# The order of loads and stores at the head of a fused transformer-block kernel: x in other parts, weights behind the transposed tiles, one store ahead of others

## The chip, the cores and the metric

The kernel runs on one core of one Trainium2 chip. The metric is the device time of one execution in microseconds (us); lower is better. Before the change the median of three runs is 823.29 us (822.75 to 823.58).

The core's engines appear under the profile's names: PE (matrix multiply), PEld (its weight load), DVE (vector), ACT (activation), POOL (general purpose) and SP, which here only issues transfers. A "q" behind a name (SPq) is that engine's instruction queue.

## The reference

The program computes the output of a pre-norm block and the gradients of its input and five weight matrices. All tensors are bf16; S = 2048 rows, D = 640, 32 heads of 20, F = 1728.

```python
def _A_ref(x, wqkv, wo):                       # linear attention
    qkv = (x @ wqkv) ...                       # q, k, v per head
    phi = lambda t: jnp.where(t > 0, t + 1, jnp.exp(t)) + 1e-6
    pq, pk = phi(q), phi(k)
    kv = jnp.einsum("bhsd,bhse->bhde", pk, v)
    z = jnp.einsum("bhsd->bhd", pk)
    num = jnp.einsum("bhqd,bhde->bhqe", pq, kv)
    den = jnp.einsum("bhqd,bhd->bhq", pq, z)[..., None] + 1e-6
    return (num / den ...) @ wo
def _B_ref(x, w1, w3, w2):                     # gated MLP
    return (silu(x @ w1) * (x @ w3)) @ w2
h  = x + _A_ref(_layernorm(x), A_wqkv, A_wo)
h2 = h + _B_ref(_layernorm(h), B_w1, B_w3, B_w2)
# outputs: h2, and by jax.vjp with grad_out the gradients of
# A_x, A_wqkv, A_wo, B_w1, B_w3, B_w2
```

## The kernel before, in words

S is cut into 16 tiles of 128 rows. D is five chunks of 128. The order of every engine's instructions is written out by hand; the framework adds the waits. No instruction overtakes another on its own engine.

The head is the stretch up to about 98 us. Three parts of it matter here.

**First pass over the tiles** (line 527, up to about 50 us). For tile t, DVE takes the statistics (`stat`, line 480, instructions of line 147), POOL makes the reciprocal deviation (line 154), and DVE or ACT normalises the tile in place (`p1_norm`, line 246; ACT for tiles 10, 12 and 14, by `on_act`). Tiles below 8 are transposed by PE (`p1_tr`) and copied by ACT (line 259). From tile 8 on the transposition is a DMA that SP issues (line 250) into `pqT`. Then PE multiplies by the k weights (`p1_mm`, line 267), ACT takes exp and relu (`phi`, lines 294 and 295), and DVE merges them in a held-back step (`rest`, lines 298 and 299), which stands as `R` in the table `v_steps` (line 508). There "S" is `stat`, "N" a norm ahead of `phi`, and "A", "B" and "L" are norms behind `phi`: "A" ahead of that iteration's `q_tile`, "B" and "L" behind it. `q_tile` does the same for the queries at iterations 6, 7, 9 and 11. All results in matrix form go to two PSUM buffers named `big`, used in turn.

SP issues x in parts (`load_x`, line 185) and the q, k and v weights in column ranges (`load_wq`, line 182: k is 2 to 4, q is 0 to 2, v is 4 to 6). The table `trickle` (line 505) hangs further weight loads on iterations: `w13` (line 499) lists loads of `w1` and `w3` for chunks (0,2), (2,4), (4,5) in the order w1, w3, w1, w3, w1, w3, and a last narrow one. `outs` (line 522) hangs stores on iterations: `group_out` stores four tiles of phi(k), `xn_out` four tiles of normalised x.

**Sums over the tiles** (lines 585 to 636, about 50 to 73 us). PE builds the matrix phi(k)^T x (`m_part`, `m_end`), whose rows SP transposes into `mT` (line 441). `kvT_block(m)` (line 443) multiplies the v weights by `mT`; block 1 needs the transposed rows of parts 1 and 2, block 2 those of parts 2 and 3. `r_T` (line 383) has the scaled query tiles transposed.

**Attention output and start of the MLP** (line 945, about 73 to 98 us). The last six query tiles (`q_late`), the product of kv and wo (`f2_wT`, transposed into `Wp`), x plus attention (`f2_half`), its layer norm (`f2_hn`, `f2_ht`), and then the MLP (`mlp`, line 783: gate by `w1`, sigmoid on ACT in line 793, up by `w3`). `q_out` (line 724) is a store, issued by POOL, of query tiles 10 to 13 from the buffer `pkx` to `pq_d`. The pool that holds `pkx` is released in line 955, and the MLP's tiles lie in the same memory, so the first sigmoid waits until `q_out` has read it.

What waits for a DMA waits for its semaphore. There are eight semaphores for the transfers that SP and ACT issue, used in turn, and a transfer waits until the one eight before it has landed.

The end of the kernel (line 1553) computes the gradients of w1 and w3 in blocks of columns; ACT copies each result out and issues its store, at first in two halves.

Of the kernel before, what the change touches and what calls it, by code (L numbers as in the profile page):

```python
# [9 lines left out]
P = 128  # L10
# [8 lines left out]
S, D, H, F = 2048, 640, 32, 1728  # L19
DH = D // H  # L20
ST, DT = S // P, D // P
# [34 lines left out]
def kernel(  # L56
# [19 lines left out]
    V, A, T, G, SY = nc.vector, nc.scalar, nc.tensor, nc.gpsimd, nc.sync  # L76
    dma, dmaT, dmaG = SY.dma_start, SY.dma_start_transpose, G.dma_start

    def rows(ap):
        return ap.rearrange("(t p) d -> p t d", p=P)  # L80
# [101 lines left out]
    def load_wq(a, b):  # L182
        dma(out=wqkv[:, :, a * HD:b * HD], in_=wq_v[:, :, a * HD:b * HD])

    def load_x(a, b):
        dma(out=x_sb[:, a:b, :], in_=xS[:, a:b, :])
# [4 lines left out]
    load_x(2, 3)  # L191
    load_wq(3, 4)
    load_x(3, 4)
    load_x(4, 8)

    mask = cp.tile([P, DT, M_MAX], BF16, name="mask")

# [25 lines left out]
    def load_g2T(c):  # L223
        g2T[c] = U2.tile([P, DT, W], BF16, name="g2T", tag="g2T", bufs=2)
        dmaT(out=g2T[c][:], in_=goD[c * W:(c + 1) * W, :])

    def load_w13(c0, c1):
        def go1():
            dma(out=w1[:, c0:c1, 0:F], in_=rows(B_w1)[:, c0:c1, :])

        def go3():
            dma(out=w3[:, c0:c1, :], in_=rows(B_w3)[:, c0:c1, 0:F - FL])
        return [go1, go3]

# [95 lines left out]
    def z_diag(m):  # L330
        dz[m] = hx[:, 10, m * P:(m + 1) * P]
        V.tensor_scalar(out=dz[m], in0=ident[:], scalar1=Z[:, m:m + 1], scalar2=None, op0=ALU.mult)
# [99 lines left out]
    def m_end(m, js=(0, 1)):  # L432
        mb = mbs[:, m % 4, :]
        acc = macc[m]
        for j in js:
            A.copy(out=mb[:, j * HD:(j + 1) * HD], in_=acc[j][:, 0:HD])
        if m < 2:
            A.copy(out=Z[:, m:m + 1], in_=acc[1][:, HD:HD + 1])
            z_diag(m)
        if m < DT - 1:  # L440
            dmaT(out=mT[:, :, m * P:(m + 1) * P], in_=mb)
# [13 lines left out]
    def load_w2T(a, b):  # L455
        dmaT(out=w2T[:, :, a:b], in_=B_w2[a:b, :])
# [1 line left out]
    zero_pads()  # L458
    load_w2T(0, 2 * P)
    load_g2T(0)  # L460
    load_x(8, 12)
    load_w2T(2 * P, 4 * P)
    load_wq(0, 2)
    load_x(12, ST)
    def warm_up(n, warm):
        for _ in range(n):
            T.matmul(warm[:, 0:P], lhsT=ones[:], rhs=ones[:], start=True, stop=True, skip_group_check=True)
# [31 lines left out]
    w13 = [go for c0, c1 in ((0, 2), (2, 4), (4, 5)) for go in load_w13(c0, c1)]  # L499
    w13 += [lambda: dma(out=w1[:, :, F:FP], in_=rows(B_w3)[:, :, F - FL:F])]  # L500

    def load_wo():
        dma(out=wo[:], in_=A_wo.rearrange("(c p) n -> p c n", p=P))

    trickle = {4: w13[0], 5: w13[1], 9: lambda: load_wq(4, 6), 12: w13[2], 14: w13[3]}

    R = None
    v_steps = {1: (R, ("N", 4)), 2: (("S", 5), R, ("N", 5)), 3: (("S", 6), R, ("N", 6), ("C", 0)),
               4: (("S", 7), R, ("N", 7), ("S", 8)), 5: (R, ("N", 8), ("S", 9)), 6: (R, ("N", 9), ("S", 10)),
               7: (("S", 11), R, R, ("A", 10), ("L", 11)), 8: (("S", 12), R, R, ("S", 13)),  # L510
               9: (("N", 13), R, ("S", 14), ("B", 12)), 10: (R, R, ("S", 15)), 11: (R, ("B", 14), ("L", 15))}
    V_OPS = {"S": stat, "N": p1_norm, "C": p1_scale}

    def xn_out(g, q):
# [4 lines left out]
        sl = slice(g * TPC, (g + 1) * TPC)  # L519
        dma(out=pk_v[:, sl, :], in_=pk_all[:, sl, :])  # L520

    outs = {7: ((xn_out, 0, dma),), 8: ((group_out, 0),), 12: ((group_out, 1), (xn_out, 1, dma)), 13: ((group_out, 2),)}

    QT = (6, 7, 9, 11)
    M0 = {7: (0, 1, 2), 8: (3, 4, 5)}
# [55 lines left out]
    def r_head(t):  # L581
        r_row(t)
        r_T(t)
# [4 lines left out]
    phi_rest()  # L588
    m_part(1, (14, 15))
    m_end(1)  # L590
    load_wo()
    group_out(SC - 1)
    for go in w13[4:]:
        go()
    z_late((2, 3, 4), big())
    m_part(2, range(10))
    z_rows(((0, 1), (2, 3, 4)), ps.tile([P, 2, 512], F32, name="bigx", tag="big", bufs=2))
# [2 lines left out]
    r_prod(1)  # L600
    m_part(2, range(10, ST))
    m_end(2)
    dmaG(out=m_v[:, 0, :], in_=mbs[:, 0, :])
    r_head(0)
    r_prod(2)
# [335 lines left out]
    def kv3():  # L941
# [3 lines left out]
    run((q_late, 10, f2_mT), (q_late, 11, kv3), (phi_rest,),  # L945
        (q_late, 12, lambda: (f2_wT(0), f2_wT(1))), (q_late, 13, lambda: (f2_wT(2), f2_wT(3))),
        (f2_wT, 4), (phi_rest,), (q_late, 14), (r_T, 4), (r_head, 5), (r_prod, 7),
        (mlp_ghh, 4),
        (q_late, 15), (w2_room,), (sig_table,), (f2_half, 0, 0), (f2_half, 1, 0), (f2_half, 2, 0), (f2_half, 3, 0), (mlp_ghh, 5),
        (f2_half, 0, 1), (r_store, 4, 5), (f2_half, 1, 1), (f2_hn, 0), (r_store, 5, 6), (f2_half, 2, 1), (f2_hn, 1),  # L950
        (f2_half, 3, 1), (f2_m_out,), (q_out, 10, 14),
        (f2_half, 4, 0, True), (mlp_ghh, 6), (f2_half, 4, 1, True), (f2_half, 5, 0, True), (r_red, 6, (0,)), (f2_hn, 2), (f2_hn, 3),
        (f2_ht, 2), (f2_ht, 3), (load_w2T, 8 * P, 10 * P), (mlp_ghh, 7), (r_red, 6, (1,)), (r_inv, 6), (r_scale, 6),
        (r_T, 6), (f2_rest,), (r_red, 7), (r_inv, 7), (r_scale, 7), (r_T, 7), (r_store, 6, 7))
# [26 lines left out]
    def r_end(t):  # L981
        r_scale(t)
        r_out(t)

    r_steps = [{0: ((load_x, 6, 8),), 1: ((r4_out, 0, 2),), 2: ((r_load, 8),), 3: ((load_w2T, 10 * P, F),), 4: ((r_load, 9), (r4_out, 2, 4)),
                5: ((r_store, 7, 8),),
                10: ((xn_out, 2, dmaG),), 12: ((r_load, 10),)},
               {0: ((r_den, 8), (load_x, 8, 12)), 1: ((r_end, 8), (r_load, 11), (xn_out, 3, dmaG)), 2: ((r_den, 9),), 3: ((r_end, 9), (r_load, 12)),
# [4 lines left out]
    for c in range(SC):  # L993
# [9 lines left out]
        for fc in range(FT):  # L1003
# [8 lines left out]
            if c == 0 and fc in (5, 7, 9, 11):  # L1012
                a, b = {5: (0, 3), 7: (3, 6), 9: (6, 10), 11: (10, 13)}[fc]
# [13 lines left out]
            if c == SC - 1 and fc in (1, 2, 5, 6):  # L1027
                i = (1, 2, 5, 6).index(fc)
# [61 lines left out]
    for fc in range(FT - 1):  # L1090
        b, i = divmod(fc, 4)
# [210 lines left out]
    a, b = ST - 1, ST - 2  # L1302
# [143 lines left out]
    for t in range(ST):  # L1446
        c, i = divmod(t, TPC)
# [105 lines left out]
    for i, (f0, f1) in enumerate(blocks):  # L1553
        n = f1 - f0
        for m in range(DT):
            last = (i, m) == (len(blocks) - 1, DT - 1)
            for a, b in ((0, n - P), (n - P, n)) if last else ((0, n),):
                c = (a + b) // 2
                halves = ((a, c), (c, b)) if i * DT + m < 5 else ((a, b),)
                out = [(x + y - a, z + y - a, to) for y, w in halves for x, z, to in both_grads(m, f0 + y, f0 + w)]  # L1560
                grad_job(hnN, m, lambda t: gb[i][:, t, a:b], b - a, out, A.dma_start)
        load_block(i + 2)
# [36 lines left out]
```

## Time and profile before

| what | value |
|---|---|
| median of three runs | 823.29 us |
| the profiled execution's own time | 820.91 us |
| its span, first to last instruction | 819.1 us |
| PE busy | 814.1 us, 99% of the span |
| DVE, ACT, POOL busy | 452.4, 323.6, 130.9 us |
| share of the chain that ended last | PE 96%, DVE 2%, ACT 1% |
| HBM read and written | 47.09 and 51.13 MB |

The profiled execution is 2.38 us shorter than the median of the runs, and 1.8 us of it lie outside the span. Busy time of PE counts a matmul from its start to its modelled end, so two that overlap are not told apart from one; whether PE lost time is read from the start of one matmul to the start of the next. All times below are from the start of the span.

### The profile page before, as it was taken

Reading aid. Unit: us, or ns where it says so; the run is one execution under the profiler, and the core shown is the slowest. Engines: PE = TensorE matmul, PEld = TensorE weight load, DVE = VectorE, ACT = ScalarE, POOL = GpSimd, SP = SyncE. Lnnn points to the kernel's source line nnn. Section 1 sums busy time; section 2 is a strip of 40 time slices with the busy share of each in tenths; the row PEclk is TensorE's granted clock in tenths of the full one; section 3 lists DMA queues with packets and bytes.
Section 4 is the critical chain, followed back from the end, with each engine's and each line's share of the span. In section 5 each row is a group of like instructions: output and inputs, shape, how many; then the busy total and the mean of one; then the engine's idle time right before and its main releaser. Section 6 shows DMA issues by size and latency. Waiting matters only on the chain.

```text
span 819.1 us, 13944 instructions
## 1 busy us (share of the span) xinstructions
PE 814.1 (99%) x5420; PEld 512.8 (63%) x5420; DVE 452.4 (55%) x973; ACT 323.6 (40%) x603; POOL 130.9 (16%) x193
## 2 busy tenths in 40 slices
PE   9999999999999999999999999999999999999998
PEld 6677544555555555777777777777777777544444
DVE  7859987998898566300057777772781544200000
ACT  7856688665565666011122212222212334211111
POOL 2233333333222212100001111110220000000000
PEclk9999999999999999999999999999999999999999
DMA  9899699796485556999977877259974997967751
GB/s 264 219 290 239 166 244 327 225 245 173 127 211 156 169 170 167 222 261 226 257 176 180 211 197 200 58 107 187 287 195 93 181 194 159 239 164 186 160 141 36
DMA packets 323873, 157.88 MB, mean 193 GB/s; under 512 B 242784, under 2 KB 317056, under 8 KB 323808
## 3 DMA queue, kind: packets, MB, share of 16 engines
q1 hardware_dynamic: 281040, 116.18, 61.6%
q0 software_dynamic: 7328, 24.48, 8.7%
q10 hardware_dynamic: 35440, 16.34, 7.7%
q8 instruction: 42, 0.69, 0.4%
q14 instruction: 23, 0.19, 0.1%
HBM read 47.09 MB, written 51.13 MB: 120 GB/s over the span
## 4 chain that ended last, share of the span: by engine, by line
PE 96%; DVE 2%; ACT 1%; issue 0%; DMA 0%; POOL 0%; ACTq 0%; DVEq 0%
PE mm L394 20%; PE job L1346 20%; PE ghn L1142 14%; PE gxn L1515 8%; PE gw L1097 7%; PE o L910 4%; PE o L856 3%; PE gwo L1230 3%; PE big L267 3%; PE gr L1199 3%; PE dkv L1452 3%; PE macc L429 2%; PE at L654 2%; PE mm L267 1%; PE dkv L1380 1%; DVE st L147 1%
## 5 line engine op out<-in xcount | busy, mean ns | idle before, releaser
L1346 PE MATMUL job<-gb,hnN 128*128 128x496 bf16 (+3 forms) x576 | 116.8, 366 | 0.0
L1142 PEld LDWEIGHTS <-ggb 128*128 128x128 bf16 x864 | 84.5, 98 | 32.8
L1346 PEld LDWEIGHTS <-hnN 128*128 128x128 bf16 x576 | 55.8, 98 | 61.0
L394 PE MATMUL mm<-pqT,w 128*128 128x512 bf16 x405 | 93.8, 379 | 0.1
L394 PEld LDWEIGHTS <-w 128*128 128x128 bf16 x540 | 52.5, 98 | 63.4 <-issue 1.4
L1350 ACT CAST obs<-job 128x496 bf16<-128x496 f32 (+4 forms) x56 | 28.5, 510 | 123.7 <-PE job L1346 120.9
L1142 PE MATMUL ghn<-w13a,ggb 128*128 128x320 bf16 x448 | 63.5, 299 | 0.0
L1157 DVE SCALAR_TENSOR_TENSOR wb<-gs,hnb 128x640 f32<-128x640 bf16 x16 | 13.2, 825 | 88.7 <-ACT gs L1154 88.7
L1142 PE MATMUL ghn<-w13b,ggb 128*128 128x320 bf16 x416 | 61.4, 299 | 0.0
L394 PE MATMUL mm<-g2T,w2T 128*128 128x512 bf16 x240 | 59.6, 379 | 0.0
L1097 PE MATMUL gw<-g,hb 128*128 128x320 bf16 x416 | 56.8, 299 | 0.0
L1207 POOL TENSOR_TENSOR sz<-Zb,g_h 128x640 f32<-128x640 bf16 x16 | 20.2, 1261 | 197.7 <-DVE g_h L1208 197.7
L1097 PEld LDWEIGHTS <-hb 128*128 128x128 bf16 x416 | 40.6, 98 | 16.0 <-issue 0.3
L419 ACT CAST ghh<-mm 128x512 bf16<-128x512 f32 x48 | 28.3, 589 | 47.7 <-PE mm L394 40.1
L793 ACT ACTIVATE sig<-mm 128x512 bf16<-128x512 f32 x56 | 33.9, 605 | 26.4 <-PE mm L394 21.1
L1154 ACT ACTIVATE gs<-ghn 128x640 bf16<-128x640 f32 x16 | 11.3, 704 | 78.8 <-PE ghn L1142 73.9
L394 PEld LDWEIGHTS <-w2T 128*128 128x128 bf16 x260 | 25.4, 98 | 23.4
L267 PEld LDWEIGHTS <-pqT 128*128 128x128 bf16 x320 | 30.7, 98 | 13.7 <-ACT pqT L259 1.5
L267 PE MATMUL big<-wqkv,pqT 128*128 128x320 bf16 x250 | 38.6, 299 | 0.6 <-ACT pqT L259 0.3
L1346 PEld LDWEIGHTS <-g 128*128 128x128 bf16 x320 | 31.0, 98 | 11.5
L829 DVE TENSOR_TENSOR gate<-gate,sig 128x1024 bf16<-128x1024 bf16 x28 | 19.3, 689 | 33.2 <-ACT gate L804 30.5
L910 PE MATMUL o<-w,hhT 128*128 128x320 bf16 x224 | 35.0, 299 | 0.0
(219 smaller groups left out, 1369.9 us busy)
## 6 DMA issues: line engine op xcount, KB each, us to landing
hh_d<-hhT SPq DMA_DIRECT2D x24, 256.0 KB, 2.7
gg_d<-gate POOLq DMA_DIRECT2D x24, 256.0 KB, 4.3
gg_d<-ghh POOLq DMA_DIRECT2D x24, 256.0 KB, 3.4
ggb<-gg_d SPq DMA_DIRECT2D x6, 896.0 KB, 5.4
ggb<-gg_d ACTq DMA_DIRECT2D x6, 832.0 KB, 5.7
ggb<-gg_d SPq DMA_DIRECT2D x2, 1728.0 KB, 12.7
x_sb<-in_A_x_dram SPq DMA_DIRECT2D x5, 640.0 KB, 5.9
pk_d<-pk_all SPq DMA_DIRECT2D x4, 640.0 KB, 6.6
```

The source lines that it names most:

```text
L267: T.matmul(acc, lhsT=pqT[:, c, t * P:(t + 1) * P], rhs=wqkv[:, c, n0:n0 + HD], start=(c == 0), stop=(c == DT - 1))
L394: T.matmul(acc[:], lhsT=w[:, c, fc * P:(fc + 1) * P], rhs=rhs[:, c, :], start=(c == 0), stop=(c == DT - 1))
L419: A.copy(out=ghh[n // 2][:, n % 2, :], in_=acc[:])
L793: A.activation(sig[:, i, :], gp[:], AF.Sigmoid)
L856: T.matmul(accs[i, j][:, 0:HD], lhsT=hhT[c][:, fc, i * P:(i + 1) * P], rhs=w2[:, fc, j * HD:(j + 1) * HD], start=(first and fc == 0), stop ...
L910: T.matmul(o2["ps"][:, 0:HD], lhsT=hhT[c][:, fc, i * P:(i + 1) * P], rhs=w2[:, fc, j * HD:(j + 1) * HD], start=(fc == 0), stop=(fc == FT - 1))
L1097: T.matmul(acc[:, j, 0:HD], lhsT=hb[b][:, t, i * P:(i + 1) * P], rhs=g2[:, t, j * HD:(j + 1) * HD], start=(t == 0), stop=(t == ST - 1))
L1142: T.matmul(acc[:, j, 0:HD], lhsT=ggb[t // 2][:, k, lo:lo + P], rhs=rhs[:, j * HD:(j + 1) * HD], start=(k == 0), stop=(k == NG - 1))
L1199: T.matmul(gr[t][:, j, 0:HD], lhsT=ghT[t][:, c, :], rhs=wT2[:, c, j * HD:(j + 1) * HD], start=(c == 0), stop=(c == DT - 1))
L1346: T.matmul(acc[:, 0:n], lhsT=lhs[:, t, m * P:(m + 1) * P], rhs=rhs(t), start=(t == 0), stop=(t == ST - 1))
L1350: A.copy(out=ob, in_=acc[:, 0:n])
L1515: T.matmul(acc[:, j, 0:HD], lhsT=g, rhs=wqT[:, k, j * HD:(j + 1) * HD], start=(k == 0), stop=(k == 14))
```

## The change

SP's, POOL's and ACT's orders change; PE's and DVE's instructions keep theirs.

- x is loaded in tiles 4 to 6, 6 to 10 and 10 to 16 in place of 4 to 8, 8 to 12 and 12 to 16.
- Of `trickle`, the load of `w3` for chunks (0,2) becomes two, one on iteration 5 and one on iteration 6. The v weights move from iteration 9 to behind `m_end(1)`. The load of `w3` for chunks (2,4) moves from iteration 14 to behind the last `group_out`. `load_wo` and the last three loads of `w13` move from there to behind `m_end(2)`.
- The first `group_out` goes from iteration 8 to iteration 9. The norm of tile 14 on ACT goes ahead of iteration 11's `q_tile`.
- `q_out` goes from behind `f2_m_out` to ahead of `mlp_ghh(4)`.
- In the first pass of the MLP, `load_w2T(10 * P, F)` and `r_load(8)` change places.
- At the end, the fifth result of the first block is stored whole, no longer in two halves.

```diff
-    load_x(4, 8)
+    load_x(4, 6)
...
-        def go3():
+        def go3(c0=c0, c1=c1):
             dma(out=w3[:, c0:c1, :], in_=rows(B_w3)[:, c0:c1, 0:F - FL])
...
     load_w2T(0, 2 * P)
     load_g2T(0)
-    load_x(8, 12)
+    load_x(6, 10)
     load_w2T(2 * P, 4 * P)
     load_wq(0, 2)
-    load_x(12, ST)
+    load_x(10, ST)
...
-    trickle = {4: w13[0], 5: w13[1], 9: lambda: load_wq(4, 6), 12: w13[2], 14: w13[3]}
+    trickle = {4: w13[0], 5: lambda: w13[1](0, 1), 6: lambda: w13[1](1, 2), 12: w13[2]}
...
-               9: (("N", 13), R, ("S", 14), ("B", 12)), 10: (R, R, ("S", 15)), 11: (R, ("B", 14), ("L", 15))}
+               9: (("N", 13), R, ("S", 14), ("B", 12)), 10: (R, R, ("S", 15)), 11: (R, ("A", 14), ("L", 15))}
...
-    outs = {7: ((xn_out, 0, dma),), 8: ((group_out, 0),), 12: ((group_out, 1), (xn_out, 1, dma)), 13: ((group_out, 2),)}
+    outs = {7: ((xn_out, 0, dma),), 9: ((group_out, 0),), 12: ((group_out, 1), (xn_out, 1, dma)), 13: ((group_out, 2),)}
...
     m_end(1)
-    load_wo()
+    load_wq(4, 6)
     group_out(SC - 1)
-    for go in w13[4:]:
-        go()
+    w13[3]()
...
     m_end(2)
+    load_wo()
+    for go in w13[4:]:
+        go()
...
         (f2_wT, 4), (phi_rest,), (q_late, 14), (r_T, 4), (r_head, 5), (r_prod, 7),
-        (mlp_ghh, 4),
+        (q_out, 10, 14), (mlp_ghh, 4),
...
-        (f2_half, 3, 1), (f2_m_out,), (q_out, 10, 14),
+        (f2_half, 3, 1), (f2_m_out,),
...
-    r_steps = [{0: ((load_x, 6, 8),), 1: ((r4_out, 0, 2),), 2: ((r_load, 8),), 3: ((load_w2T, 10 * P, F),), 4: ((r_load, 9), (r4_out, 2, 4)),
+    r_steps = [{0: ((load_x, 6, 8),), 1: ((r4_out, 0, 2),), 2: ((load_w2T, 10 * P, F),), 3: ((r_load, 8),), 4: ((r_load, 9), (r4_out, 2, 4)),
...
-                halves = ((a, c), (c, b)) if i * DT + m < 5 else ((a, b),)
+                halves = ((a, c), (c, b)) if i * DT + m < 4 else ((a, b),)
```

## The prediction

> **What bounds the kernel now.** I read the page first, then the chain of waits from 0 to 110 us, then the timelines of PEld, SP and ACT there, and the list of DMA issues for single transfers.
>
> ```profile
> PE 814.1 (99%) x5420; PEld 512.8 (63%) x5420; DVE 452.4 (55%) x973; ACT 323.6 (40%) x603; POOL 130.9 (16%) x193
> ...
> PEclk9999999999999999999999999999999999999999
> ```
>
> PE is busy 99% of 819.1 us at full granted clock, and the change leaves its 5420 matmuls alone. So a gain can only come from places where PE starts a matmul late, and a loss only from new ones. The chain shows two in the head:
>
> ```profile
> 35.83 0.50 DVE pk_all L299
> 36.37 0.37 issue
> 36.73 0.70 ACT mq L294
> 37.44 0.60 ACT rq L295
> 38.08 1.52 PE big L267 x10
> ...
> 95.78 0.37 POOL m_d L712
> 96.15 2.67 DMA pq_d<-pkx
> 98.82 1.86 issue
> 100.79 0.04 issue
> 100.84 0.46 ACT sig L793
> ...
> 102.45 4.48 PE mm L394 x20
> ```
>
> The first: DVE's merge of an earlier tile releases ACT, ACT's relu frees the buffer `big`, and PE starts at 38.08. From 25 us to there the chain is DVE almost without a gap. The second: `q_out`, issued at 96.15, lands at 100.6 (4.5 us in the list of issues), and only then may the first sigmoid overwrite `pkx`; its matmul had ended at 99.10. PE then waits for ACT's copy out of its PSUM buffer. The timeline of the weight loads has the places in PE's own row:
>
> ```profile
> 38.09 1.18 PEld L267 LDWEIGHTS <-pqT 128*128 128x128 bf16 x9 [0.32 <-issue]
> ...
> 40.12 1.32 PEld L267 LDWEIGHTS <-pqT 128*128 128x128 bf16 x10
> ...
> 97.83 4.23 PEld L394 LDWEIGHTS <-w 128*128 128x128 bf16 x21 [0.46 <-issue]
> 102.45 1.61 PEld L394 LDWEIGHTS <-w 128*128 128x128 bf16 x8 [0.40 <-issue]
> ```
>
> From start to start, against the usual 0.136 us (320 columns) and 0.216 us (512), PE loses 0.28 us at 38.08, 0.16 at 97.86 and 0.28 at 102.45. The row at 40.12 lost nothing, but its tile 12 landed at 37.03 + 3.0 = 40.0: met by 0.1 us. So are tile 9 (25.81 + 4.6 = 30.46, wanted at 30.60) and tile 14 (41.79 + 2.6 = 44.36, wanted at 44.47).
>
> **x in other parts.** Tiles 6 and 7 used to land with tiles 4 and 5 at 9.70; now they come with the second part, issued in the place that SP reached at 11.25, and `stat(6)` wants them at 15.74:
>
> ```profile
> 7.08 4.12 SPq L225 DMA_TRANSPOSE g2T<-in_grad_out_dram  x1
> 11.25 0.58 SPq L186 DMA_DIRECT2D x_sb<-in_A_x_dram  x1
> ...
> 15.74 0.88 DVE L147 BATCH_NORM_STATS2 st<-x_sb 128x6 f32<-128x320 bf16 x2
> ```
>
> The 640 KB part of before took 4.8 us from there: 16.07, 0.33 us too late. But 4.12 us for `g2T`'s issue is long (2.66 at 552.70 for as many rows): SP stood behind a backlog, and that is now 320 KB smaller, 0.97 us by the old part's own pace (landings 7.76 to 9.70 for 640 KB). So it issues between 10.28 and 11.25 and lands between 15.1 and 16.07. Earlier data gain nothing, as DVE is not free before 15.74. A delay d costs little at first (the transposition of tile 6 is ready 0.49 us early) but DVE has no gap to recover in, so d arrives at 38.08 in full. Bounds 0 to +0.33; I take 0, since the row of `g2T` says that SP waited for the queue. The Trainium skill, "DMA: Bandwidth & Descriptors", section "Anatomy of one DMA", fits 2.0 us plus bytes over 436 GB/s (for POOL's transfers): an estimate of 3.5 us, landing at 14.75 even from 11.25, and so 0 at both ends. The row's 4.8 us, for SP's transfer, says that this is too short here. The last part, now 960 KB, lands some 0.9 us after the old 22.5; `stat(10)` starts at 25.70: 0.
>
> **Weights and transposed tiles.** Half of `w3`, 416 KB, leaves the place ahead of tile 9 and stands ahead of tile 10, whose 32.42 has until 34.13; 416 KB took about 1.0 us (832 KB, landings 58.03 minus 55.95). The first `group_out` no longer stands ahead of tiles 13 and 12, nor 800 KB of v weights ahead of tile 14. Margins grow by 0.4 to 1.1 us, time by 0. ACT's norm of tile 14 (0.94 us) goes ahead of the last `q_tile`'s exp and relu: its buffer frees at 41.9 and not 40.96, PE wants it at 42.43: 0.
>
> The v weights now go where `wo` was issued (55.35, 6.5 us): 61.9, for a matmul at 64.10; the slowest loads near there took 9.0 us, which would be 64.35 and cost 0.25. I take 0, from the same size in the same place. Part 2 of `mT` has only 0.4 us in hand (68.08 for 68.48) and loses `wo` and three loads from ahead of it: not later. Part 3 (68.28 + 5.5 = 73.76, wanted at 75.64) gets them ahead, 1.88 us in hand. What is really new in SP's queue there is the 800 KB, some 2.1 us, moved out of a slack stretch. Engines were 43% busy at 69 us, so it partly fills room: bounds 0 to +0.2, I take 0. `wo`, by 72 for 78, and the last w loads, by 73 for 97.83, have room. SP's issues behind them (the `r_T` tiles) are read after 85.
>
> **`q_out` earlier.** POOL reaches it behind `r_prod(7)`, at 84.42 + 1.54 = 85.96; it costs POOL 0.76 us, with its next work at 91.72. With the 4.5 us of before it lands at 90.5, well ahead of the sigmoid. The sigmoid then starts behind its matmul, near 99.15 and not 100.84; ACT's copy comes 1.7 us earlier and the 0.28 us at 102.45 go. Next in line there is PE itself. At 97.86 the transposed tile 1 took 3.4 us where 2.6 is usual; but `q_out` was issued 1.8 us behind it and two stores stay, so of 0.16 I take 0.05 (bounds 0 to 0.16).
>
> Its price is a collision where it now runs, 87 to 90 us, with the last transposition of `Wp` (85.22, 2.6 us, 1.4 us in hand) and two `r_T` tiles (over 3 in hand). Bounds 0 to +1.5: the 480 KB store issued at 68.36 made its neighbour 2.9 us late, and 2.9 minus 1.4 is 1.5. I take 0, as that store moved its bytes only about 2 us after its issue; here that is 88, when the `Wp` tile has landed (87.84). The same page, "Queues, rings and completion order", says that an engine alternates between queues packet by packet; by that rule the tile would be held at most twice its own time, under its 1.4 us, and again 0. The trace does not bear it out well: at 71 to 72 us POOL's store moved nearly all the bytes.
>
> **The rest.** The load of `w2T`'s last rows landed at 119.21 for 119.79; issued ahead of `r_load(8)` it gains room; the latter is read much later: 0. One store fewer near 716 us saves ACT a 0.34 us issue beside matmuls that do not wait: 0.
>
> **Sum.** -0.28 - 0.05 = -0.33 us: span 818.8, the execution 820.91 - 0.33 = 820.6. The median of the runs stands 2.38 above the profiled execution; I carry that over: 823.29 - 0.33 = 823.0. About 0.2%, 1.65 us, is what a measurement of this kernel tells from no change, so this is "same". The bounds, the collision aside, give 822.85 (all of the 0.16) to 823.8 (0.33, 0.25 and 0.2 on top); with the runs' own spread of 0.4 to either side the forecast's own range is 822.4 to 824.2.
>
> **Rivals.** (1) *Margins that hold only in this execution.* Tiles 9, 12, 14 and tile 1 of the MLP are met by 0.10 to 0.14 us. If the 2.38 us of the other runs are mostly such waits, growing with any slower transfer, the change removes most of them: 2.0 us, 821.3. For: all runs are slower than the profiled one, and every such margin grows. Against: 1.8 us of that execution lie outside the span too, so the difference may be the way of timing; no row shows such a wait.
>
> (2) *Slower: tile 6 late.* It decides as soon as the second x part lands after 15.74. The transfers right behind it took 6.8, 7.5 and 8.6 us; at 6.8 from 11.25 it lands at 18.05, DVE is 2.3 us late, nothing in its row makes it up, and PE loses that by 38.08: 823.29 + 2.3 - 0.33 = 825.3. Against: those stood behind this one, it stands behind less than before.
>
> (3) *`q_out` in the wrong company*: `Wp`'s tile as late as the bound says, +1.5 - 0.33: 824.5.
>
> (4) *The sigmoid is held by something else*: the 0.28 us stay, 823.3. Its other waits had ended long before, so this is unlikely.
>
> **Chances.** Forecast 0.50, (1) 0.27, (2) 0.15, (3) 0.04, (4) 0.04. Faster by over 0.2%: (1), 0.27. Slower: (2), 0.15. Within: the rest, 0.58. The range goes from 821.0, which takes in (1), to 824.8, which takes in (3) and the bounds and leaves out most of (2).
>
> **What would show it.** Right: the first sigmoid near 99.2 with no DMA in the chain ahead of it, no gap in PEld near 102.2, `q_out` at 86, `stat(6)` at 15.74 in an unbroken DVE row, 0.28 still lost at 38. Wrong: DVE waiting for x near 15.7 and over 0.3 us lost at 38; a gap of PEld at 64, 68, 75 or 89; a median more than 1.65 us away while the span moved by 0.3.

## The result, and the profile after

| what | before | after |
|---|---|---|
| median of 9 runs each, alternating | 822.86 us (821.97 to 826.29) | 820.81 us (820.24 to 822.61) |
| ratio after / before, 95% interval | | 0.9977 (0.9968 to 0.9987) |
| profiled execution: span | 819.1 us | 818.8 us |
| profiled execution: own time | 820.91 us | 820.60 us |

The change makes the kernel 2.05 us faster, which is more than the 1.65 us that can be told from no change. The profiled execution moved by 0.31 us, nearly the 0.33 us of the forecast, but out of other parts than the forecast's (below). Most of the gain is therefore in what the other executions of the kernel before do and its first profiled one did not.

The page of after: PE's busy time is again nearly the whole span (some matmul records are missing in this trace).

```profile
PE 812.4 (99%) x5393; PEld 513.0 (63%) x5420; DVE 452.7 (55%) x973; ACT 323.8 (40%) x603; POOL 130.9 (16%) x193
```

The chain of waits of after, 30 to 110 us. Both stretches shown of before are now PE alone: no DVE or ACT ahead of `big` near 38, no DMA and no ACT between the transposed rows (96.45) and the end of the first two MLP steps.

```profile
36.52 2.72 PE big L267 x20
39.23 0.82 PE macc L429 x6
...
96.45 0.45 PE trh L767 x5
96.90 5.18 PE mm L394 x24
102.13 4.48 PE mm L394 x20
```

The timeline of PE's weight loads of after. The 20 loads from 36.22 run on where 9 of them began with a gap at 38.09 before; the row at 97.60 has 30 loads without a gap. In between stands a wait that before did not have, ahead of 85.55.

```profile
36.22 2.68 PEld L267 LDWEIGHTS <-pqT 128*128 128x128 bf16 x20
...
85.55 2.57 PEld L656 LDWEIGHTS <-pqT 128*128 128x128 bf16 x20 [0.65 <-issue]
...
97.60 6.36 PEld L394 LDWEIGHTS <-w 128*128 128x128 bf16 x30
```

Three rows of the timelines of SP, DVE and ACT: the second x part is issued at 10.68 (11.25 before), tile 6's statistics start unhindered at 15.65, and the first sigmoid starts at 99.14 behind ACT's own copy (100.84 before, behind the store).

```profile
10.68 0.58 SPq L186 DMA_DIRECT2D x_sb<-in_A_x_dram  x1
...
15.65 0.88 DVE L147 BATCH_NORM_STATS2 st<-x_sb 128x6 f32<-128x320 bf16 x2
...
99.14 0.60 ACT L795 ACTIVATE sig<-mm 128x512 bf16<-128x512 f32 x1 [0.21 <-ACT x_sb L661]
```

Weight load by weight load against before, the profiled execution gains 0.09 us at the start, 0.27 at 38, loses 0.51 at 85.5 and gains 0.45 between 96 and 102. Only the last of these stood in the forecast's sum, as 0.33, so that the agreement of the totals is luck.

### The profile page after: what moved, and what is told of

Same layout as the page of the kernel before. It is cut to its first block, busy times and chain, and to the rows that moved or that the text cites. A ratio compares the mean times of both kernels' runs of the same rounds, so it can differ in the third digit from the quotient of the medians.

```text
span 818.8 us, 13921 instructions
## 1 busy us (share of the span) xinstructions
PE 812.4 (99%) x5393; PEld 513.0 (63%) x5420; DVE 452.7 (55%) x973; ACT 323.8 (40%) x603; POOL 130.9 (16%) x193
## 4 chain that ended last, share of the span: by engine, by line
PE 97%; ACT 1%; DVE 1%; issue 0%; POOL 0%; DVEq 0%; ACTq 0%
PE mm L394 20%; PE job L1348 20%; PE ghn L1144 14%; PE gxn L1517 8%; PE gw L1099 7%; PE big L267 4%; PE o L912 4%; PE o L858 3%; PE gwo L1232 3%; PE macc L429 3%; PE gr L1201 3%; PE dkv L1454 3%; PE at L656 2%; PE dkv L1382 1%; PE gp L394 1%; PE warm L467 0%
```

## The experiments

Eighteen runs were made in five groups. Each group ran on one chip with the kernel before among it (medians of before: 822.62, 822.68, 823.12, 823.13 and 823.72 us), and each run left one profile. The main reading is the same for all: the k-th weight load of the kernel's profile against the k-th of the first profile of before, and in which stretch the difference changed. The table gives these changes in us (plus is lost time; stretches by the first profile's clock; "sigmoid" is 95 to 106). "Close" is the time from the last store's landing to the end of the span, beyond the 1.2 us of before. (e4's own time is 2.15 us above its span, so that its execution did not end earlier.)

| kernel | start to 25 | tile 9, 30.6 | 38 | tile 14, 44.5 | mT, 68 | Wp, 85 to 90 | sigmoid | 107 to 540 | 540 to 568 | close | own time of that execution |
|---|---|---|---|---|---|---|---|---|---|---|---|
| before, first profile | 0 | 0 | 0 | 0 | 0 | 0 | 0 | 0 | 0 | 0 | 820.91 |
| e1_again (before) | 0.02 | 1.40 | -0.27 | 0 | 0.48 | 0 | 0.83 | 0 | 0 | 0 | 823.39 |
| h1_before (before) | 0.07 | 1.20 | -0.28 | 0 | 0 | 0 | 0.64 | 0.37 | 0.01 | 0 | 822.93 |
| e2_store | -0.02 | 1.22 | -0.28 | 0 | 0 | 0 | -0.45 | 0 | 0.01 | 0 | 821.42 |
| e3_weights | 0.33 | 0 | 0.03 | 0 | 0 | 0 | 0.90 | 0 | 0.01 | 0.41 | 822.59 |
| e4_x | 0.22 | 1.42 | -0.28 | 0 | 0.07 | 1.33 | 0.60 | 0 | 0.01 | -0.29 | 824.38 |
| after, first profile | -0.09 | 0 | -0.27 | 0 | 0 | 0.51 | -0.45 | 0 | 0 | 0 | 820.60 |
| f1_after (after) | -0.07 | 0 | -0.27 | 0 | 0 | 0 | -0.45 | 0 | 0.01 | 0 | 820.12 |
| g4_after (after) | 0.06 | 0 | -0.24 | 0 | 0 | 0 | -0.45 | 0 | 2.10 | 0 | 822.38 |
| h2_after (after) | -0.01 | 0 | -0.19 | 0 | 0 | 0.16 | -0.45 | 0 | 0.35 | 0 | 820.77 |
| f2_after_store_back | 1.68 | 0.37 | -0.09 | 0 | 0 | 0 | 0.79 | 0 | 0.52 | 0 | 824.22 |
| f3_half_w3_and_store | -0.04 | 0 | 0.01 | 0 | 0.30 | 0 | -0.45 | 1.19 | 0.01 | 0.41 | 822.35 |
| f4_after_loads_back | 0.32 | 0 | -0.15 | 2.07 | 0 | 0 | -0.45 | 0 | 0.79 | 0 | 823.52 |
| g1_x_back | -0.06 | 0 | 0.03 | 0 | 0 | 0.28 | -0.45 | 0 | 0.01 | 0 | 820.65 |
| h3_x_back_again | 0.41 | 0 | 0.03 | 0 | 0 | 0 | -0.45 | 0 | 1.53 | 0 | 822.42 |
| g2_x_and_store_back | 0.09 | 0 | 0.03 | 0 | 0 | 0 | 0.04 | 0 | 0.44 | 0 | 821.46 |
| g3_x_after_tile_six | 0.08 | 0 | 0.02 | 0 | 0 | 2.13 | -0.46 | 0 | 0.01 | 0 | 822.70 |
| h4_rows_of_x_later | 0 | 0 | 0.02 | 0 | 0 | 0 | -0.45 | 0 | 0 | 0.43 | 820.95 |
| i1_rows_of_x_close (as h4) | -0.04 | 0 | 0.02 | 0 | 0 | 0 | -0.45 | 0 | 0.01 | 0.43 | 820.89 |
| i2_half_w3_close (as f3) | 0.94 | 0 | -0.28 | 0 | 0 | 0 | -0.45 | 0 | 0.01 | 0.43 | 821.58 |

### First group: the kernel before again, and each part of the change alone

**The kernel before, unchanged.** 

> The kernel before, unchanged, once more: it tells how far two sets of runs of one kernel differ, and gives a second profiled execution. Theory M (the just-met transfers of the head turn into waits in most executions): ratio 1.000, and if the execution profiled is a usual one (span near 821, not 819.1), PE starts late by 0.2 us or more at one or several of tile 9, 12 or 14 in the first pass, at tile 1 of the MLP, or behind the first sigmoid, about 2 us in total more than in the first profile. Theory E (the extra lies elsewhere, at the start or the end of the kernel, and the change touches it by chance): ratio 1.000, the head between 20 and 110 us as in the first profile, the extra at another place.

Measured: 822.53 us (821.85 to 825.53), ratio 1.0004 (0.9995 to 1.0013). In its timeline of weight loads PE waits for tile 9, and longer at 104.91 than the first profile did at 102.45:

```profile
32.14 2.56 PEld L267 LDWEIGHTS <-pqT 128*128 128x128 bf16 x20 [1.56 <-DMA pqT<-x_sb]
...
104.91 3.98 PEld L394 LDWEIGHTS <-w 128*128 128x128 bf16 x19 [1.17 <-issue]
```

Its chain of waits names both transfers. The transposition of tile 9 was issued at 25.83 (25.81 in the first profile) but took 6.27 us and not 4.65, behind the 832 KB of `w3` issued at 24.66. The store `q_out` is issued at 97.76; the 2.67 and 2.70 us are its 5.3 us to landing.

```profile
25.83 6.27 DMA pqT<-x_sb
32.09 0.04 issue
32.14 1.94 PE big L267 x13
...
97.76 2.67 DMA pq_d<-pkx
100.43 2.70 issue
```

So the first profile of before was an execution that happened to lose little. Theory M is borne out for tile 9 and the sigmoid; tiles 12 and 14 cost nothing here. Another 0.48 us went at part 2 of `mT`, which the first profile met by 0.4.

**The store alone.**

```
-        (mlp_ghh, 4),
+        (q_out, 10, 14), (mlp_ghh, 4),
...
-        (f2_half, 3, 1), (f2_m_out,), (q_out, 10, 14),
+        (f2_half, 3, 1), (f2_m_out,),
```

> Before, with q_out alone moved ahead of mlp_ghh(4). Theory S (the store's landing holds the first sigmoid, and in most executions by much more than the 0.28 us of the first profile): most of the gain, ratio 0.998 (-1.5 us or more). Theory M (the transposed tiles): only the 0.3 us of the forecast, ratio 0.9996.

Measured: 821.89 us (821.42 to 822.33), ratio 0.9990 (0.9981 to 0.9998). That is 0.73 below before in its group, half of what theory S asked for and more than theory M's 0.3. Nothing is lost at the sigmoid, but tile 9 still costs 1.22:

```profile
31.92 2.56 PEld L267 LDWEIGHTS <-pqT 128*128 128x128 bf16 x20 [1.38 <-DMA pqT<-x_sb]
```

**The weights alone** (halves of `w3`, v weights, fourth block of `w3`, `wo` and the last w loads later, first `group_out` one iteration later, norm of tile 14 ahead of the last `q_tile`; the lines of the last two are left out here).

```
-    trickle = {4: w13[0], 5: w13[1], 9: lambda: load_wq(4, 6), 12: w13[2], 14: w13[3]}
+    trickle = {4: w13[0], 5: lambda: w13[1](0, 1), 6: lambda: w13[1](1, 2), 12: w13[2]}
...
-    load_wo()
+    load_wq(4, 6)
...
-    for go in w13[4:]:
-        go()
+    w13[3]()
...
+    load_wo()
+    for go in w13[4:]:
+        go()
```

> Before, with the moves of the w3, v, wo and w loads, the first group_out one tile later and the norm of tile 14 ahead of the last q_tile; x parts and q_out as before. Theory M: most of the gain, ratio 0.998 to 0.9985 (-1.2 to -1.7 us), PE without a gap at tiles 9, 12 and 14. Theory S: 0, ratio 1.000, with the gap behind the first sigmoid as before.

Measured: 822.40 us (821.50 to 824.34), ratio 0.9998 (0.9989 to 1.0007): 0.22 us, not theory M's 1.2 to 1.7. Tile 9 landed at 29.36 and cost nothing, as theory M said; the sigmoid cost 0.90, and 0.41 us stand at the close:

```profile
103.71 3.98 PEld L394 LDWEIGHTS <-w 128*128 128x128 bf16 x19 [1.45 <-issue]
```

**The x parts alone.**

```
-    load_x(4, 8)
+    load_x(4, 6)
...
-    load_x(8, 12)
+    load_x(6, 10)
...
-    load_x(12, ST)
+    load_x(10, ST)
```

> Before, with x loaded in tiles 4 to 6, 6 to 10 and 10 to 16, nothing else. Theories M and S: 0, ratio 1.000. The forecast's bounds: 0 to +0.33 us. If this part carries the gain (a third theory X: the statistics or g2T come sooner and DVE's unbroken chain to 38 us starts sooner), ratio 0.998.

Measured: 822.81 us (822.04 to 825.13), ratio 1.0003 (0.9993 to 1.0013): no gain. The profile loses at tile 9 and the sigmoid like the other executions of before, and 1.33 at `Wp`, with the weight loads in their old places:

```profile
88.19 2.57 PEld L654 LDWEIGHTS <-pqT 128*128 128x128 bf16 x20 [1.48 <-DMA Wp<-pkx]
```

So no part gives the whole 2 us, and the parts do not simply add: where tile 9 was late, the 0.28 us at 38 was not lost as well (e1, e2; h1 below), because PE came later to the buffer that it would have waited for.

### Second group: the change without a part, and the two parts that the first group names

**The changed kernel, unchanged.** 

> The changed kernel, unchanged, for a second profile and more runs. Theory T (the kernel before usually loses 1.2 to 1.4 us at 30.6 behind the undivided 832 KB load of w3, and 0.6 to 0.9 us at the first sigmoid behind the store of the turned queries; the changed kernel loses neither): 820.8, tile 9 lands by 29.5, no gap of PE at 30.5 or at 102, the mT tiles met, and the gap of about 0.5 us at 85.5 is there again, since SP's queue brings the Wp tile late in every execution. Theory L (luck: the one profile of the changed kernel was as lucky as the first one of the kernel before): a gap of over 0.5 us somewhere between 28 and 82, and 821.5 or more.

Measured: 820.97 us (820.12 to 823.43), ratio 0.9986 (0.9977 to 0.9995). No gap at tile 9 or the sigmoid, and none at 85.5 either: the gap there is not in every execution, against what theory T expected. Five of the twelve times lie above 822, seven below 821.3.

**The store back in its place.**

```
-        (q_out, 10, 14), (mlp_ghh, 4),
+        (mlp_ghh, 4),
...
-        (f2_half, 3, 1), (f2_m_out,),
+        (f2_half, 3, 1), (f2_m_out,), (q_out, 10, 14),
```

> The changed kernel with q_out back in its old place, all else as changed. Theory T: the store takes 0.6 to 0.9 us again at the first sigmoid, but the gap at 85.5 stays (it was SP's transposition, not the store), so 821.5 and a gap in PE near 102. Theory C (the store at 85.5 was itself what held the Wp tile): the gap at 85.5 goes, 0.5 back, so 821.0. Theory W (the store's place is worth only the 0.28 us of the first profile): 821.1 with the gap at 85.5 still there.

Measured: 821.14 us (820.58 to 824.22), ratio 0.9986 (0.9976 to 0.9995). The sigmoid costs 0.79 again in the profile, which is the slowest of the twelve executions; the lowest time is only 0.46 above that of f1, so there are executions in which the store's old place costs less than 0.5. The profile also shows what the prediction's second rival described: the second x part, issued at 10.87, landed at 18.00, and DVE and PE waited (timelines of DVE and of the weight loads):

```profile
18.02 0.89 DVE L147 BATCH_NORM_STATS2 st<-x_sb 128x6 f32<-128x320 bf16 x2 [2.23 <-DMA x_sb<-in_A_x_dram]
...
20.59 0.28 PEld L257 LDWEIGHTS <-x_sb 128*128 128x128 bf16 x5 [1.87 <-DVE x_sb L160]
```

**Before, with halves of w3 and the store alone.**

```
-    trickle = {4: w13[0], 5: w13[1], 9: lambda: load_wq(4, 6), 12: w13[2], 14: w13[3]}
+    trickle = {4: w13[0], 5: lambda: w13[1](0, 1), 6: lambda: w13[1](1, 2), 9: lambda: load_wq(4, 6), 12: w13[2], 14: w13[3]}
...
-        (mlp_ghh, 4),
+        (q_out, 10, 14), (mlp_ghh, 4),
```

> The kernel before with two parts of the change alone: the second block of w3 loaded in two halves (416 KB behind tile 8, 416 KB behind tile 9) and q_out moved. Theory T: both usual losses go, 822.6 - 1.3 - 0.7 = 820.6; and as the v weights, wo and the last w loads stay in their old places, the gap at 85.5 does not come, or seldom. Theory E (the other moved loads carry part of the gain): 821.3 or more, with gaps of PE at tiles 10 to 14 (34 to 45) or at mT part 2 (68.5).

Measured: 821.49 us (820.85 to 825.11), ratio 0.9993 (0.9983 to 1.0003): not the 820.6 of theory T. Tile 9 landed at 29.07 and the sigmoid waited for nothing, but `mT` part 2 was late by 0.30, behind `wo` and three more loads, and 1.19 us were lost near 131 to 135, which did not come back in i2 below:

```profile
68.87 0.30 PEld L448 LDWEIGHTS <-wqkv 128*128 128x128 bf16 x5 [0.46 <-DMA mT<-hx]
```

**The change with its late loads back.**

```
-    trickle = {4: w13[0], 5: lambda: w13[1](0, 1), 6: lambda: w13[1](1, 2), 12: w13[2]}
+    trickle = {4: w13[0], 5: lambda: w13[1](0, 1), 6: lambda: w13[1](1, 2), 9: lambda: load_wq(4, 6), 12: w13[2], 14: w13[3]}
...
-    load_wq(4, 6)
+    load_wo()
...
-    w13[3]()
+    for go in w13[4:]:
+        go()
...
-    load_wo()
-    for go in w13[4:]:
-        go()
```

> The changed kernel with the v weights, the fourth block of w3, wo and the last w loads back in their old places (x parts, halves of w3, q_out and the rest as changed). Theory T: the gap at 85.5 came from SP standing behind the loads that were put near 61 to 72; without them 820.3, and x(0,6) is issued before 77 and its landing is no longer at 83.5. Against it, wo and three loads stand ahead of mT part 2 again, which was met by 0.4 in one profile and missed by 0.5 and 0.2 in two: if that is the usual case 820.6 to 820.8, no better than the change. Theory P (the Wp tile is late by chance, whatever SP carries): a gap near 85.5 here too, 820.8.

Measured: 821.80 us (821.40 to 823.52), ratio 0.9992 (0.9984 to 1.0001). Worse than the change, by 0.8 us against f1. No gap at 85.5, but the v weights stood ahead of tile 14 again (issued at 39.42), and it took 5.70 us where 2.6 is usual. Its chain of waits:

```profile
41.10 5.70 DMA pqT<-x_sb
46.80 0.05 issue
46.84 1.26 PE big L267 x8
```

In the seven profiles that have the v weights there and tile 14's norm in its old place, the tile took 2.57 to 2.64 us. There its transposition was issued 3.5 to 4.5 us behind the v weights; in f4 it was 1.68, since the norm comes earlier, and the first `group_out`, now on iteration 9, stood right ahead of the weights. So tile 14 was on time in all of these; as far as one profile tells, it is the earlier norm and the later `group_out` that want the weights gone from there.

### Third group: x in its old parts

**The change with the old parts of x.** Diff: the three `load_x` lines as in before. 

> The changed kernel with x loaded in its old parts (4 to 7, 8 to 11, 12 to 15), all else as changed. Theory D (tile 6's statistics, wanted at 15.7, wait for the new second part in a share of the executions: 2.2 us and 1.7 lost by PE in one profile, 0.3 lost in two, nothing in two; so the changed kernel's times of 822.1 and more are these executions): the lowest stays at 820.1 to 820.6, hardly any time above 821.5, the median 0.2 to 0.5 lower than that of the changed kernel in the same call, 820.5, and stat(6) starts near 15.7. Theory N (the new parts relieve the queue and help the weights behind them): stat(6) near 15.7 as well, but the median 821.3 or more, with a gap at tiles 9 to 14.

Measured: 820.64 us (820.33 to 820.87, seven runs), ratio 0.9974 (0.9963 to 0.9985), with no time above 820.9. The profile loses 0.28 at `Wp` and, with the old parts, the 0.28 at 38 is there:

```profile
38.05 1.18 PEld L267 LDWEIGHTS <-pqT 128*128 128x128 bf16 x9 [0.34 <-issue]
...
85.67 2.57 PEld L656 LDWEIGHTS <-pqT 128*128 128x128 bf16 x20 [0.43 <-issue]
```

**Old x parts and the old place of the store.** Diff: that of g1 and that of f2. 

> The changed kernel with both the x parts and q_out as they were: the moved weights, the halves of w3 and the earlier norm of tile 14 are left. Theory T and D (wait at tile 9, at tile 14 and at the sigmoid): g1 plus 0.5, so 821.0; a gap near 102 of 0.6 to 0.9 us. Against it stands the run of the moved weights without the norm of tile 14, 822.4. Theory N (the new x parts are what the gain needs): 822.2 or more.

Measured: 822.21 us (821.05 to 823.71), ratio 0.9989 (0.9978 to 0.9999). That is 1.57 above g1 on the same chip, with the store's place as the only difference; the 821.0 expected was too low. (The run that the expectation sets against it, e3, had the norm of tile 14 moved as well, so g2 is e3 with the whole store at the end and the exchanged loads, and both agree: 0.91 below before here, 0.22 and the 0.43 of the close there.) Its one profile lost as little at the sigmoid as the first profile of before did (store issued 96.27, landed 4.50 us later).

**x in parts of tiles 4 to 6, 7 to 10 and 11 to 15.**

```
-    load_x(4, 6)
+    load_x(4, 7)
...
-    load_x(6, 10)
+    load_x(7, 11)
...
-    load_x(10, ST)
+    load_x(11, ST)
```

> The changed kernel with x in parts of tiles 4 to 6, 7 to 10 and 11 to 15: the first tile of the second part is wanted at 18.4 and not at 15.7. Theory D: a landing of 15.4 to 18.0 is in time, so as g1: 820.5, hardly any time above 821.5. Theory N: as the changed kernel or better, 820.8, for the parts stay spread. If both kernels with another tile 6 keep a tail above 822, that tail is not tile 6's.

Measured: 820.87 us (820.52 to 822.70), ratio 0.9977 (0.9968 to 0.9986). The median is as theory D had it, but three of eleven times are above 821.5, and the profile is one of them. It shows the third rival: `q_out`, issued at 86.00, ran together with the last transposition of `Wp`, issued at 85.97, which took 5.59 us and not 2.6; the third one was late too.

```profile
86.77 2.57 PEld L656 LDWEIGHTS <-pqT 128*128 128x128 bf16 x20 [1.40 <-DMA Wp<-pkx]
91.60 0.52 PEld L656 LDWEIGHTS <-pqT 128*128 128x128 bf16 x5 [1.12 <-DMA Wp<-pkx]
```

**The changed kernel beside them.** 

> The changed kernel on the same chip, as the measure for g1 to g3 and for a third profile: 820.9, with times in two groups, near 820.5 and near 822.3. In its profile the x part lands between 15.3 and 18; if the run is of the upper group, the 1.7 us must stand in PE between 16 and 21 (theory D) and not behind 25.

Measured: 821.28 us (820.25 to 822.55), ratio 0.9981 (0.9970 to 0.9992). Its profile is of the upper group, but against theory D not because of tile 6: x landed at 15.83, and the 2.10 us stand far outside the change, at 566, where PE waits for `tri`. The transposition it waits for was issued at 562.64 and took 5.48 us, 2.62 in the first profile of before; POOL issued a store 1.23 us behind it (timelines of SP and POOL):

```profile
562.64 1.22 SPq L1239 DMA_TRANSPOSE tri<-tri  x1
...
563.87 0.60 POOL L1354 DMA_DIRECT2D out_dram<-obs  x1 [14.14 <-ACT obs L1352]
```

### Fourth group: more profiles, and SP's queue ahead of Wp

**The kernel before again.** 

> The kernel before, unchanged, for a third profile. Theory T: 822.7; a gap of 1.2 to 1.4 us at tile 9 near 30.6 (it was there in all three executions with the undivided w3 load but the first), and 0.6 to 1.1 at the sigmoid. Theory L (the first profile is the usual one): no gap at 30.6, at most 0.28 at the sigmoid, and the rest of the 822.7 somewhere the change does not touch, for instance at 547 to 567, where other kernels lost up to 2.1 us.

Measured: 822.75 us (821.51 to 824.12), ratio 0.9997 (0.9988 to 1.0006). The third profile of before loses in the two places that the second one did (timelines of the weight loads and of ACT). Theory L falls.

```profile
31.99 2.56 PEld L267 LDWEIGHTS <-pqT 128*128 128x128 bf16 x20 [1.36 <-DMA pqT<-x_sb]
...
102.47 0.60 ACT L793 ACTIVATE sig<-mm 128x512 bf16<-128x512 f32 x1 [2.66 <-PE mm L394]
```

The matmul named there had long ended; the store had landed at 102.25.

**The changed kernel again.** 

> The changed kernel once more: 820.8 to 821.3, lowest 820.2, some 3 in 10 of the times above 822; no gap at 30.6 or at 102; if above 821.5, the loss is at tile 6 (16 to 19), at Wp (85 to 90) or at 547 to 567.

Measured: 821.15 us (820.27 to 823.55), ratio 0.9979 (0.9969 to 0.9988); three of twelve above 822, as expected. Its profile loses 0.16 at `Wp` and 0.35 at 566.

**Old parts of x again.** 

> The changed kernel with the old parts of x, again: theory D (tile 6 makes the tail) 820.6, hardly any time above 821.5, lower than h2 by 0.2 to 0.6. If the tail is Wp's or that of 547 to 567, which have nothing to do with x, it shows here too: 3 in 10 above 822, and the median that of h2.

Measured: 820.95 us (820.38 to 823.09), ratio 0.9976 (0.9967 to 0.9985), with two of eleven above 822. So the upper times are not tile 6's alone: this profile (822.42) lost 1.53 us at 566. The list of waits has it:

```profile
PE gkvT L1401 <- DMA tri<-tri: 1.4, 1, 1.4
```

**Two of six tiles of x behind the transpositions of Wp** (on top of g1).

```
-    load_x(0, 6)
+    load_x(0, 4)
...
-        (f2_wT, 4), (phi_rest,), (q_late, 14), (r_T, 4), (r_head, 5), (r_prod, 7),
+        (f2_wT, 4), (phi_rest,), (q_late, 14), (r_T, 4), (load_x, 4, 6), (r_head, 5), (r_prod, 7),
```

> As h3, and of the six rows of x that SP loads ahead of the transpositions of Wp, two (tiles 4 and 5, 160 KB) go behind them. Theory Q (Wp is late since it stands behind that load in SP's queue): the load ahead lands about 0.4 to 0.8 us sooner, Wp's third tile by 85.2 and not 85.5, the gap of 0.3 at 85.6 goes: 820.3, 0.3 under h3. Theory C (Wp's tiles are late by the store of the turned queries or by chance): the gap near 85.6 stays or moves to 91, no gain on h3.

Measured: 821.20 us (820.80 to 823.75), ratio 0.9981 (0.9973 to 0.9990). In the profile the load ahead landed at 82.35 and not 83.61 (g1), `Wp`'s third tile at 85.20 and not 85.61, and there is no gap at 85.5, as theory Q said. That alone proves little, since h3, without this edit, had none either. But the twenty profiles bear theory Q out. Corrected for the time that PE had lost or gained by then, the tiles of x loaded ahead landed at 83.54, 83.64, 83.87, 84.63 and 84.87 in the five that lose at `Wp`'s third tile (h2, g1, after, g3 and e4, which lose 0.16, 0.28, 0.51, 1.26 and 1.33), and at 83.42 or earlier in the fifteen others. The third tile landed 1.8 to 2.0 us behind them in all five. But 820.3 did not come: the lowest of twelve times is 820.80, where g1 and h3 had 820.33 and 820.38. The weight loads lose nothing more; 0.43 us stand behind the last store instead, and the fifth group asks why. Rows of SP's timeline:

```profile
77.14 1.40 SPq L186 DMA_DIRECT2D x_sb<-in_A_x_dram  x1
79.93 6.49 SPq L708 DMA_TRANSPOSE Wp<-pkx  x5
...
88.85 0.70 SPq L186 DMA_DIRECT2D x_sb<-in_A_x_dram  x1
```

### Fifth group: the time behind the last store

**The kernel of h4 again** (diff as there). 

> The kernel of h4 once more, for the time between the last store's landing and the end of the span. Theory K (it belongs to the kernel): 1.6 us again, lowest time 820.8. Theory R (it belongs to the execution): 1.2 us, and a time of 820.4 or less where the weight loads lose nothing. In both, no gap at 85.5.

Measured: 821.06 us (820.82 to 822.92, eight runs), before in this group 823.72 us, ratio 0.9970 (0.9957 to 0.9984). The span ends 1.63 us after the last landing again, which is theory K. `Wp`'s third tile lands at 85.19, and there is no gap at 85.5.

**The kernel of f3 again** (diff as there). 

> The kernel of f3 once more, for the same time at the end. Theory K: 1.6 us again, lowest time 820.8; theory R: 1.2 us. Beside it: tile 9 lands near 29.1 and costs nothing, and the 1.19 us lost near 131 to 135 in f3 show whether they come back.

Measured: 821.72 us (821.09 to 823.46, eight runs), ratio 0.9987 (0.9974 to 1.0000). 1.63 us again: theory K. Tile 9 landed at 29.03 and cost nothing; 0.94 us were lost at 14.4 to 15.4, where PE waited for `g2T`, which landed at 15.34 (13.22 in the first profile of before).

The traces' semaphore events show what the time is. At the end SP waits for all transfers in eight steps, in a fixed order of their semaphores: 101 first, then 104 to 110. In the kernel before, the change and the kernels not named below, SP and ACT issue 424 transfers, and the last store has semaphore 110. The first seven steps are then over before it lands, and one is left. In e3, f3 and h4 the halved `w3`, or the second load of x, makes it 425. The last store then has semaphore 101, SP stands at the first step until it lands, and takes the other seven behind it at 0.06 us each: 7 x 0.061 = 0.43 us. The change itself halves `w3` (one transfer more) and stores one result at the end in one piece (one fewer), so it stays at 424.

## Why the prediction was right or wrong

**The step that failed: "The median of the runs stands 2.38 above the profiled execution; I carry that over."** The 2.38 us were not a way of timing. Every execution's time stands some 1.8 us above its span, the profiled ones included (1.7 to 2.2), and the other executions of before really are longer: two more profiles of it show 823.39 and 822.93. They lose it in waits for transfers, as rival (1) had it, but only in part in those that the rival named. Tile 9, met by 0.1 us in the first profile, costs them 0.9 to 1.1 us net; tiles 12 and 14 cost nothing. The store, which already cost the first profile 0.45, costs 0.64 and 0.83 more, and one of them loses 0.48 at a part of `mT` that the first profile met by 0.4, the other 0.37 behind 107. The rival's chance was 0.27 and its time 821.3; measured 820.81, also below the range's 821.0. Of the 2.2 us between the forecast of 823.0 and this, 0.43 is the base: nine runs of before have a median of 822.86, where three had 823.29.

**Tile 9, "met by 0.1 us" and counted as 0.** The condition was right, the price was missing. With the undivided load of 832 KB the tile was late in four of five executions (e1, e2, e4, h1), by 1.20 to 1.42 us for PE; with the halves it was late in none of fifteen, landing 3.1 to 3.4 us after its issue against 6.1 to 6.3. The 0.28 us at 38 come back in exchange, unless x is in the new parts, so about 1.0 us net.

**The store, -0.33.** Right in direction, and 0.45 in the first pair of profiles: the 0.28 at 102.45 as foreseen, and the 0.16 at 97.86 in full where 0.05 was taken. The sigmoid's new start agrees to 0.01 us (99.14 against the 99.15 foreseen) by luck, since the 0.51 lost at `Wp` cancelled the gains ahead of it. But in its old place the store landed within 4.5 us of its issue only in the first profile of before (4.46) and in g2 (4.50); in e1, e3, e4, f2 and h1 it took 5.06 to 5.36, and the gain against those executions is 1.05 to 1.35 us. This term was mis-sized from one execution too. By medians the store's place is worth 0.7 (e2), 0.2 (f2 against f1) and 1.6 (g2 against g1); how often its old place costs the larger amount stays open.

**"0.28 still lost at 38".** Wrong: it was gone, or smaller, in every execution with the new parts of x (after, e4, f1, f2, f4, g4, h2) and there in g1, g2, g3, h3, h4, i1, e3 and f3, which have other parts. It was gone with the old parts too in e1, e2, h1 and i2, where PE had lost 0.9 to 1.4 us before it and came later. Where PE had lost less than 0.1 by then, the parts alone divide the profiles: gone or smaller in four with the new ones (after, f1, g4, h2), there in seven with others (the first profile, f3, g1, g2, g3, h4, i1). So it is the x parts that do it; how is not shown. ACT's exp at that place starts 0.10 us behind the end of DVE's merge in f1 and 0.42 behind it in g1, with DVE's row the same.

**x, "bounds 0 to +0.33; I take 0".** Right for the usual execution: in six of the seven profiles with these parts, the second one landed at 15.37 to 16.22, and PE lost nothing by it before 30 us. The row of `g2T`, whose issue shrank from 4.12 to 3.35 us, bore out the smaller backlog. In f2 it landed at 18.00, and PE lost 1.71 us at once and 0.37 near 32, close to the 2.3 of rival (2). (The 0.3 us that the expectation of g1 puts down to tile 6 in two other profiles was lost before 12 us, and h3 and e3 lose as much there with the old parts.) By the fit that the Trainium skill, "DMA: Bandwidth & Descriptors", section "Anatomy of one DMA", gives for POOL's transfers, the estimate for this part was 3.5 us; for SP's transfer the runs show 4.84 to 7.13.

**Weights and late loads, 0.** Margins grew as argued (tile 9 landed 1.5 us ahead of its need, tile 14 1.0, the first profile after). What was missing is that they would be needed, at tile 9 in the kernel before and at tile 14 once its norm comes earlier (f4 lost 2.07 there). The other side was missed as well. Part 3 of `mT` had 0.28 us in hand and not 1.88 (landed 74.99, wanted 75.27), and behind the 800 KB and `wo` SP's queue brought the six tiles of x 1.1 us later (83.50 against 82.39), and with them `Wp`'s third tile: 0.51 us in the first profile, 0.16 in h2, none in f1 and g4. The moved loads are not the only thing that can make x late: e4 lost 1.33 there without them.

**The collision of the store and Wp, bound 1.5, taken as 0.** No loss in the four profiles of the changed kernel. g3 lost 2.13 us, but 1.26 of that was the late third tile; the collision cost 0.88, within the bound. It follows from the other loss: the late third tile held the issue of the last one back until `q_out` came 0.03 us behind it. In the twelve other profiles with the store in its new place, `q_out` was issued 0.64 to 0.98 us behind the last transposition of `Wp`, and this took 2.6 us. From the rule that an engine alternates between queues packet by packet (the Trainium skill, "DMA: Bandwidth & Descriptors", section "Queues, rings and completion order") the prediction took a delay of the tile under 1.4 us; in g3 the last tile was 3.0 us late. From 89 to 90 us the store's queue moved 0.40 MB there, and SP's next to nothing.

**One store fewer near 716 us, taken as 0.** Wrong by 0.43 us beside the halved `w3`, and the halves by as much the other way, so that the sum did not show it: the unchanged count of 424 transfers keeps the close short. The fifth group shows the close at 425; the change with its store in two halves was not run.

**What the parts add up to.** Medians against before in the same group: store -0.7; weights -0.2; x +0.2; `w3` halves with the store -1.2 and -2.0; the change without x -2.5 and -2.2; the change -1.7, -1.8 and -2.0. Without the 0.43 us of the close, the weights give -0.65 and the halves add 0.9 to the store (f3 against e2), which is the 1.2 to 1.4 of tile 9 less the 0.28 at 38. The rest of the change seems to keep what the halves and the store win: a wait that is removed brings every later need forward, and tile 14, `mT` part 2 and `Wp` were the next to be late (f4, f3, g3). That is argued from single profiles; the intervals of e3, f3 and i2 reach to 1.0 or beyond. The kernels without the new x parts were the best run: 820.64 and 820.95, where the change had 821.28 and 821.15 in the same groups, and with two tiles of x behind `Wp` 821.20 and 821.06, 1.9 and 2.7 us under before in their groups and with 0.43 us of close still in them. All beat the kernel before; that they beat the change is likely for the first, but the intervals overlap. The last one with one transfer fewer was not tried.

## What to carry to other kernels

Before costing an edit from a trace, set the profiled execution's time beside the median of the runs: where the profiled one is shorter by more than the runs' spread, the missing time can be waits that this trace doesn't show, and the first suspects are the transfers that it met by a few tenths of a microsecond or waited for a little. A second profile of the same kernel settles it. Bulk loads behind the small transfers that the next matmul needs, and in halves, can be worth it even where a trace shows no wait. And a removed wait brings every later deadline forward, so look for the next transfer with little in hand, here the one whose queue took the moved loads; and count the transfers, since one more or less can change what the kernel waits for at its end.

## What the runs showed of the hardware

- The same transfer at the same place in SP's queue takes very different times from execution to execution: tile 9 behind 832 KB took 4.65 us once and 6.08 to 6.27 four times, and the 640 KB of the second x part 4.84 to 5.19 us six times and 7.13 once.
- A margin that decides nothing in most executions can cost the most of all: PE waits for `tri` at 566 us, far behind the change, lost 0.35 to 2.10 us in six of twenty profiles and 0.01 or less in the others, where the tile landed 1.35 to 1.75 us ahead of its weight load. One thing divides them: in the six, POOL issued its next store 1.23 to 1.76 us behind this transposition, which then took 4.19 to 5.48 us; in the fourteen the store came 1.86 to 2.18 us behind it, and it took 2.57 to 2.65. How the store does it, if it does, is not shown. The six are among the twelve profiles of kernels that were made from the change, none among the eight of the kernel before and those made from it; whether the change makes this wait likelier was not tried.
- The order in which the end of the program waits for semaphores is worth 0.43 us here: 424 transfers leave 1.18 to 1.22 us behind the last landing (0.91 in e4) and 425 leave 1.61 to 1.63, since the eight semaphores are used in turn and the count decides which one the last store has.
